# Softmax sums completed on VectorE, and output clearings tied to late pair loads, in a one-core attention and mixture-of-experts kernel

## The chip, the cores and the metric

The kernel runs on one core of one Trainium2 chip. The metric is the device time of one execution in microseconds (us), as the median of three runs. TensorE (PE) multiplies matrices, VectorE (DVE), ScalarE (ACT) and GpSimd (POOL) work element by element, and SyncE (SP) issues most of the memory transfers; GpSimd issues the indexed ones, which gather or scatter rows by a list of numbers. Each engine takes its instructions strictly in the order of its own queue, so an instruction that waits holds up everything behind it on that engine.

## The reference

Attention over eight batches of 576 positions with eight heads of 64, each position seeing itself and the 127 before it, and then a layer of eight experts of which every token takes the two best:

```python
scores = np.where(mask, scores + bias[None], -1000000000.0)
scores = scores - np.max(scores, axis=-1, keepdims=True)
attn = np.exp(scores)
attn = attn / (np.sum(attn, axis=-1, keepdims=True) + 1e-09)
...
noisy_logits = logits + noise_scale * noise
top2 = np.argpartition(-noisy_logits, 2, axis=1)[:, :2]
...
h = np.maximum(x[mask] @ w1[e], 0.0)
out[mask] += top2_w[mask, k, None] * (h @ w2[e])
```

## The kernel before, in words

The first part is attention. Its 32 pairs (a batch and two of its heads) are loaded one after the other (`qk`, line 452), each into one of four buffers. A pair is worked in three groups of query blocks: blocks 0 and 1, blocks 2 and 3, and the half block 4. A group passes through scores on PE (L498, or L491 for block 4), mask and maximum on DVE (L519, L524), the exponential on ACT, which leaves each row's sum in the tile `den` (L531), a transposition on PE (L538), its copy out of the bank by ACT or DVE (L266 or L270, tile `pT`), a split by two masks on GpSimd (L558, L559), and the product with the values on PE (L579).

When the four pairs of a batch have passed for one group, `rows` finishes it. The sums in `den` get 1e-9 added and are inverted. For block 4 the two heads of a pair lie on top of each other in the partitions, so that the sums of the lower half are first moved beside those of the upper half. Transposed rows (L681) are then multiplied by the inverted sums (L684) and stored as tokens in `xs`, and `gate` computes the experts' logits (L706, L717, L722, and the sum over heads on GpSimd, L731 and L732).

When a batch has all its logits, `route` picks two experts for every token, counts them (L782 to L787), makes lists (L822, L829) and adds them to the table `slots` in memory by an indexed transfer of GpSimd (`scatter`, L895 and L896). After the sixth batch (`CUT`) the first 768 tokens of expert 0 are gathered (L1157), made into two half-precision parts, turned by transposing transfers of SP (L1202) and fed to the first feed-forward blocks (L1210 up, L1254 down), which stand on PE between the last pieces of attention. The second part is feed-forward alone. Results are added to `out` by indexed transfers (L1343).

`out` and the spare rows of `xs` have to be cleared before that. `set_ups` does it with eleven transfers of 1 MB from a tile of zeros (L428), one after the other: one into `xs`, ten into `out`.

No queue's order is written by hand. A planner (`Order`) walks through all strands of work at build time with a cost for each piece and a rank that says which piece goes first; what it decides becomes the order of the queues. The ranks come from the numbers at the top (`LOAD` and `VALUES` for the loads of pairs and values, `GATE`, `ROUTE` and `SCATTER` for the end of a batch, `STAGE` for the steps of a group, `LATE` for choices between ACT and DVE).

Of the kernel before, what the change touches and what calls it, by code (L numbers as in the profile page):

```python
# [14 lines left out]
OP = mybir.AluOpType  # L15
# [3 lines left out]
B, H, S, D = 8, 8, 576, 64  # L19
# [17 lines left out]
NTR = 512  # L37
NPAD = N + NTR
BLOCKS = tuple(((FROWS, c - FROWS),) if z < NF else ((0, 512), (512, 384), (896, c - 896)) for z, c in enumerate(CAPS))
ZERO = 61.9  # L40
LOAD = -46.8
VALUES = 27.7
GATE = (-11.1, 102.8)
ROUTE = (6.1, 22.2)
SCATTER = (1.3, -1054.0, -21.3)
FFN0, FFN1 = 174.1, 232.3
WEIGHTS = (101.9, 86.4)
TOKENS = 85.5
STAGE = (-3.5, 6.3, 21.9, -7.2, 18.8, 32.3, 14.3, -20.1)
MIDDLE = 51.1  # L50
RESULT = -82.8
SIZES = (62.8, 73.0, 959.3)
SOON = 22.0
TIGHT = (1, 5, 7)
QUICK = (5, 7)
LATE = (-6.5, -40.7, 56.9, 77.5, 0.4, -92.0, 49.5, -132.3, 49.1, -25.4, 8.5, -39.8)
LAG = 0.2
TURN, MARGIN, LATE_BY = (1.4, 0.3), 1.0, 1.0
PACE, READ_BY, AHEAD = 4.0, 2.0, 16
HELD = 3  # L60
SWITCH, NEAR = 0.093, 6.2
TOP, SOFT, SPLIT = (1.27, 1.52, 0.46), (1.56, 1.56, 0.4), (0.85, 1.35, 0.6)
SP_COST = 0.45
DMA_RATE = 300e3
# [162 lines left out]
def attention_moe(ctx: ExitStack, tc: tile.TileContext, qk_, v, w_gate, w_noise, noise, w1, w2,  # L227
                  out, xs, slots, eye):
    nc = tc.nc
# [23 lines left out]
    def dve(us, rank, emit, join=True):  # L253
        return Op((("DVE", us, rank),), emit, join)

    def pool(us, rank, emit, join=True):
        return Op((("POOL", us, rank),), emit, join)
# [14 lines left out]
    def move(size, rank, emit):  # L272

        end = yield Op((("SP", SP_COST, rank),), emit)
        yield order.transfer(end, size)
# [12 lines left out]
    PAIRS = B * NP  # L288
# [84 lines left out]
    def set_ups():  # L373
        def small():
            nc.gpsimd.memset(base, 0)
            nc.gpsimd.memset(rest_of_line, 0)
            nc.gpsimd.memset(wgn, 0.0)
            for t in lgs:
                nc.gpsimd.memset(t, 0.0)
            nc.gpsimd.memset(caps, float(CAP))  # L380
            nc.gpsimd.memset(takes, 0.0)
            nc.gpsimd.iota(names, pattern=[[0, NQ], [1, E]], base=0, channel_multiplier=0,
                           allow_small_or_imprecise_dtypes=True)
            nc.gpsimd.memset(names[64:128, 4, :], 100.0)
            nc.gpsimd.iota(starts_, pattern=[[SPAN * LINE // 128, E]], base=0, channel_multiplier=0,
                           allow_small_or_imprecise_dtypes=True)
            nc.gpsimd.iota(iota8, pattern=[[1, E]], base=0, channel_multiplier=0,
                           allow_small_or_imprecise_dtypes=True)

        def counts_():  # L390
            for t, pattern, first_, step in ((steps_, [[1, E * SPAN]], 0, 0), (numbers, [[128, NQ]], 1, 1),
                                             (spare, [[128, 4]], N, 1), (mine, [[-SPAN, E]], 0, 1)):
                nc.gpsimd.iota(t, pattern=pattern, base=first_, channel_multiplier=step,
                               allow_small_or_imprecise_dtypes=True)
            nc.gpsimd.memset(numbers[64:128, 4:5], 0.0)
            nc.gpsimd.iota(first_line, pattern=[[0, 1]], base=0, channel_multiplier=1,
                           allow_small_or_imprecise_dtypes=True)

        def columns():
            reached = tmp[0:E * SPAN, 0]  # L400
            nc.vector.tensor_scalar(reached, mine, 0.0, None, op0=OP.is_ge)
            nc.vector.tensor_reduce(tmp[0:E * SPAN, 1, 0:1], reached[:, 1:E], axis=AX.X, op=OP.add)
            nc.vector.scalar_tensor_tensor(first_line, tmp[0:E * SPAN, 1, 0:1], float(LINES - SPAN), first_line,
                                           op0=OP.mult, op1=OP.add)
            nc.vector.scalar_tensor_tensor(mine, mine, float(SPAN), reached, op0=OP.is_lt, op1=OP.mult)
            nc.vector.tensor_copy(line_of[0], first_line)
            nc.vector.tensor_scalar(least[:, 0], iota8, float(NF), float(FROWS), op0=OP.is_lt, op1=OP.mult)

        yield pool(0.4, 2, small)
        yield pool(0.6, 4, counts_)  # L410
        yield pool(0.46, 5, lambda: nc.gpsimd.memset(zero, 0.0))
        for z, w in enumerate((w_gate, w_noise)):
            for h in range(2):
                yield from move(2e4, 6, lambda w=w, z=z, h=h: nc.sync.dma_start(
                    wgn[h * D:h * D + D, :, h * 16 + z * E:h * 16 + z * E + E],
                    dram(w, h * D * E, [[E, D], [128 * E, 4], [1, E]])))
        yield from move(2e5, 7, lambda: nc.sync.dma_start(noi, noise))
        yield dve(0.8, 7, columns)
        nt = E * EROWS // 128
        yield from move(2e5, 8, lambda: nc.sync.dma_start(dram(slots, 0, [[nt, 128], [1, nt]]), zero[:, 0:nt]))  # L420
        yield from move(1e4, 8, lambda: nc.sync.dma_start(eye, ident[0:E, 0:E]))
        mark(set_up)
        rest_ = NTR // 128 * XW - 4 * DM
        yield from move(2e4, 16, lambda: nc.sync.dma_start(
            dram(xs, N * XW + 4 * DM, [[4 * DM + rest_, 128], [1, rest_]]), zero[:, 0:rest_]))
        for z, (ap, r) in enumerate([(xs, N * XW)] + [(out, r * DM) for r in range(0, NPAD, 512)]):
            row_ = 4 * DM + (0 if z else rest_)
            yield from move(1e6, 16 + ZERO * z, lambda ap=ap, r=r, row_=row_: nc.sync.dma_start(  # L428
                dram(ap, r, [[row_, 128], [DM, 4], [1, DM]]), zero[:, None, :].to_broadcast([128, 4, DM])))
        put(xgr, zeros)  # L430
        mark(emptied)
# [5 lines left out]
    loaded = [Event() for _ in range(PAIRS)]  # L437
# [5 lines left out]
    def loads():  # L443

        for k in range(PAIRS):
            rank = 5 * k - LOAD
            t = qks[k] = yield (qkr, rank)
# [7 lines left out]
    def all_values():  # L455
        for y in range(2 * B):
            rank = 10 * y - VALUES
            if y == 0:
# [133 lines left out]
    def unit(u):  # L592
        k, gr = units[u]
        blocks = GROUPS[gr]
        t = k * NQ + blocks[0]
        r0, r1, r2, r3, r4, r5, r6, r7 = (t + z for z in STAGE)
        b, g, y = k // NP, k % NP, k // 2
# [40 lines left out]
        if g == NP - 1:  # L638
            spawn(rows(b, gr, t))
# [3 lines left out]
    def rows(b, gr, t):  # L643

        yield filled[b, gr]
        blocks, den = GROUPS[gr], dens[b, gr]
        nr, nz = 64 if blocks == (4,) else 128, len(blocks)
        rank = t - GATE[b + 1 == CUT]

        def sums():  # L650
            if nz == 1:
                nc.gpsimd.tensor_copy(den[0:64, 0, 1:H:2], den[64:128, 0, 0:H:2])
            nc.gpsimd.tensor_scalar(den[0:nr, 0:nz], den[0:nr, 0:nz], 1e-9, None, op0=OP.add)

        yield pool(0.4 if nz == 1 else 0.2, rank, sums)
        yield dve(0.2, rank, lambda: nc.vector.reciprocal(den[0:nr, 0:nz], den[0:nr, 0:nz]))
        done = Event(nz + 1)
        spawn(gate(b, blocks, xus[b, gr], den, t, done))
        for z, i in enumerate(blocks):
            spawn(row_major(b, i, xus[b, gr][:, :, z * 128:z * 128 + nr], den[0:nr, z], t + z, done))  # L660
        yield done
        put(xur[nz == 1], xus[b, gr])
        put(denr, den)
# [8 lines left out]
    def row_major(b, i, xu, den, t, done):  # L672

        rank = t - GATE[b + 1 == CUT]
        rows = 64 if i == 4 else 128
# [19 lines left out]
    def gate(b, blocks, xu, den, t, done):  # L695


        rank = t - GATE[b + 1 == CUT]
        nz, i = len(blocks), blocks[0]
# [51 lines left out]
    def route(b):  # L751
# [146 lines left out]

        rank = 20 * b + SCATTER[2 if b == B - 1 else b + 1 == CUT]
        yield pool(1.08, rank, scatter)  # L900
# [151 lines left out]
    def say(e):  # L1052
# [6 lines left out]
        yield begun[e - 1]  # L1059
        yield Op((("SP", 1.5, SIZES[2] + step_of(e) - 1),), load)  # L1060
        mark(known[e])
# [9 lines left out]
    def early_sizes():  # L1071

        yield biased[NP - 1]
        for e in range(EARLY):
            done = Event(16)
            for f in range(8):
                for z, (rg, src) in enumerate(((raw1, w1), (raw2, w2))):
                    t = yield (rg, SIZES[e])
                    v = t.rearrange("p a b -> p (a b)") if z == 0 else t
                    spawn(largest(rg, t, v, (0.6, 0.7)[z], SIZES[e], wam[:, e % 2, z, f:f + 1],  # L1080
                                  dram(src, e * DM * F + f * 65536, [[512, 128], [1, 512]]), done, z))
            yield done
            yield from powers_of_weights(e, SIZES[e])

# [149 lines left out]
    def middle(blk, f, t, rank, end):  # L1234
        c = blk.n
        yield end
        if f == 7:
# [4 lines left out]
        blk.h[f][1].extend((hh, hl))  # L1242
        yield either(0.052 + c * 0.000833, 0.067 + c * 0.00104, rank - MIDDLE, LATE[8], lambda e: relu(
            e, hh[:, 0:c], t[:, 0:c]))
        yield dve(0.07 + c * 0.00104, rank - MIDDLE, lambda: nc.vector.scalar_tensor_tensor(  # L1245
            hl[:, 0:c], t[:, 0:c], 0.0, hh[:, 0:c], op0=OP.max, op1=OP.subtract))
# [114 lines left out]
    def first_tokens():  # L1361
        for z, blk in enumerate(first):
            yield from tokens(blk, ranks1[8 * z] - TOKENS)

# [257 lines left out]
```

## Time and profile before

| | |
|---|---|
| Median of three runs | 1075.29 us (1074.47 to 1076.39) |
| Profiled execution, its own time | 1074.38 us |
| Span of its profile, first to last instruction | 1072.6 us |
| Busy: PE, DVE | 1025.2 us (96%), 681.9 us (64%) |
| Busy: ACT, GpSimd | 444.4 us (41%), 391.1 us (36%) |
| Mean granted PE clock | 0.982 of 2.4 GHz |

The time is 1.8 us longer than the span. The shares are averages over two parts with different habits: in the first 275 us all four compute engines work on attention, afterwards PE is almost never idle. The granted clock is the share of 2.4 GHz that PE was given; 0.50 stands for 1.2 GHz.

### The profile page before, as it was taken

The page shows a single profiled execution, that of the slowest core. Times are in us where ns is not written, and L with a number is a line of the kernel's source. Part 1 is how long each engine was busy: PE and PEld are TensorE (multiplying, and loading weights), DVE is VectorE, ACT ScalarE, POOL GpSimd, SP SyncE. Part 2 cuts the span into 40 slices and gives each one's busy share as a digit, 9 for nine tenths or more (in the row PEclk, how much of TensorE's full clock was granted, in tenths as well). Part 3 has the DMA queues.
Part 4 walks back from the last instruction along what each step waited for, and adds up shares of the span by engine and source line. Part 5 has one row for each costly group of instructions (what it writes and reads, how often), then busy time and mean ns, then how long its engine had stood idle before and what let it go on. Part 6 is the DMA issues. An engine that isn't in the chain of part 4 may idle for free. (4 is left out here: it accounts for less than half of the span.)

```text
span 1072.6 us, 20479 instructions
## 1 busy us (share of the span) xinstructions
PE 1025.2 (96%) x6880; PEld 604.6 (56%) x6880; DVE 681.9 (64%) x2402; ACT 444.4 (41%) x1265; POOL 391.1 (36%) x660
## 2 busy tenths in 40 slices
PE   8997997888998999999999999999999999999996
PEld 5765665555554554564457456645744574574454
DVE  8987996678747765665666676546755664673311
ACT  8986785556223342333333234314423331442211
POOL 4466775676442130332213142205222330431112
PEclk9999998899999999999999999999999999999998
DMA  8889785525368994979479868948894797787113
GB/s 304 303 293 315 224 304 186 157 71 145 91 169 185 181 193 132 192 126 219 101 151 213 187 79 188 190 132 170 141 241 63 180 187 184 139 132 90 23 35 48
DMA packets 193307, 178.62 MB, mean 167 GB/s; under 512 B 104048, under 2 KB 147344, under 8 KB 193200
## 3 DMA queue, kind: packets, MB, share of 16 engines
q1 hardware_dynamic: 175856, 138.34, 48.0%
q0 software_dynamic: 17344, 38.94, 22.7%
q8 instruction: 55, 0.90, 0.4%
q14 instruction: 52, 0.43, 0.1%
HBM read 117.29 MB, written 40.71 MB: 147 GB/s over the span
## 5 line engine op out<-in xcount | busy, mean ns | idle before, releaser
L1343 POOL DMA_INDIRECT out_dram<-yo,ix x71 | 114.9, 1618 | 504.3 <-ACT yo L266 491.9
L1230 ACT ACTIVATE hh<-bank 128x384 f16<-128x384 f32 (+9 forms) x177 | 87.6, 495 | 435.3 <-PE bank L1210 415.5
L1245 DVE SCALAR_TENSOR_TENSOR hl<-bank,hh 128x384 f16<-128x384 f32 (+9 forms) x192 | 107.8, 561 | 233.3 <-ACT hh L1230 225.6
L1254 PEld LDWEIGHTS <-hh 128*128 128x128 f16 x912 | 89.2, 98 | 96.2
L1210 PE MATMUL bank<-xh,w1hb 128*128 128x512 f16 (+8 forms) x384 | 126.5, 329 | 0.0
L1210 PE MATMUL bank<-xl,w1hb 128*128 128x512 f16 (+8 forms) x384 | 126.5, 329 | 0.0
L1210 PE MATMUL bank<-xh,w1lb 128*128 128x512 f16 (+8 forms) x384 | 126.4, 329 | 0.0
L531 ACT ACTIVATE p<-p,nm 128x128 f32<-128x128 f32 x288 | 111.7, 394 | 14.9 <-DVE nm L524 14.8
L1210 PE MATMUL bank<-xl,w1ha 128*128 128x384 f16 (+8 forms) x320 | 105.6, 330 | 0.0
L1210 PE MATMUL bank<-xh,w1la 128*128 128x384 f16 (+8 forms) x320 | 105.6, 330 | 0.0
L1210 PE MATMUL bank<-xh,w1ha 128*128 128x384 f16 (+8 forms) x320 | 105.6, 330 | 0.0
L1210 PEld LDWEIGHTS <-w1hb 128*128 128x128 f16 x768 | 74.8, 98 | 53.7
L1210 PEld LDWEIGHTS <-w1ha 128*128 128x128 f16 x768 | 74.6, 98 | 53.6 <-issue 0.3
L1157 POOL DMA_INDIRECT xg<-xs_dram,ix x71 | 79.7, 1123 | 40.7 <-issue 13.9
L1254 PE MATMUL bank<-w2ha,hl 128*128 128x512 f16 x228 | 86.6, 380 | 3.3 <-DVE hl L1245 1.8
L1254 PE MATMUL bank<-w2hb,hl 128*128 128x512 f16 x228 | 86.5, 380 | 0.2 <-DVE hl L1245 0.2
L1254 PE MATMUL bank<-w2hb,hh 128*128 128x512 f16 x228 | 86.5, 380 | 0.0
L1254 PE MATMUL bank<-w2ha,hh 128*128 128x512 f16 x228 | 86.5, 380 | 0.0
L1254 PE MATMUL bank<-w2lb,hh 128*128 128x512 f16 x228 | 86.5, 379 | 0.0
L1254 PE MATMUL bank<-w2la,hh 128*128 128x512 f16 x228 | 86.5, 379 | 0.0
L579 PE MATMUL bank<-pT,vraw 128*64 128x128 f32 (+2 forms) x896 | 76.1, 308 | 10.5 <-POOL pT L559 7.7
L1115 DVE TENSOR_REDUCE wam<-mraw 128x1 f32<-128x1024 f32 x56 | 66.9, 1210 | 21.0 <-DMA mraw<-in_w_dram 21.0
(242 smaller groups left out, 2029.7 us busy)
## 6 DMA issues: line engine op xcount, KB each, us to landing
raw<-in_w_dram SPq DMA_DIRECT2D x144, 256.0 KB
mraw<-in_w_dram SPq DMA_DIRECT2D x56, 512.0 KB
qk<-in_qk_dram SPq DMA_DIRECT2D x32, 608.0 KB
vraw<-in_v_dram SPq DMA_DIRECT2D x16, 640.0 KB
out_dram<-xg SPq DMA_DIRECT2D x10, 1024.0 KB
xs_dram<-x SPq DMA_DIRECT2D x32, 256.0 KB
xg<-xs_dram,ix POOLq DMA_INDIRECT x71
xh<-th SPq DMA_TRANSPOSE x71
```

The costliest lines, as they stand in the source:

```text
L531: nc.scalar.activation(pv, pv, AF.Exp, bias=nm[:, z, h:h + 1], scale=-1.0, accum_out=den[:, z, 2 * g + h:2 * g + h + 1])
L579: nc.tensor.matmul(o[half, o0:o0 + c], t[:, kb, hh:hh + D], w, start=m == 0, stop=m == len(lst) - 1)
L1115: yield dve(us, rank, lambda: nc.vector.tensor_reduce(o, v, axis=AX.X, op=OP.max, apply_absolute_value=True))
L1157: yield pool(1.04, rank, lambda: nc.gpsimd.indirect_dma_start(out=xg[0:r], out_offset=None, in_=xs[0:blk.rows], in_offset=bass.IndirectOff ...
L1210: nc.tensor.matmul(t[:, 0:blk.n], wp[:, c], x[:, c, 0:blk.n], start=c == 0 and z == 0, stop=c == 3 and z == 2)
L1230: nc.scalar.activation(o, i, AF.Relu)
L1245: yield dve(0.07 + c * 0.00104, rank - MIDDLE, lambda: nc.vector.scalar_tensor_tensor(hl[:, 0:c], t[:, 0:c], 0.0, hh[:, 0:c], op0=OP.max, ...
L1254: nc.tensor.matmul(blk.y[j][0:r], h[:, cs], wp, start=f == 0 and m == 0, stop=f == 7 and m == 2)
L1343: ins = nc.gpsimd.indirect_dma_start(out=out, out_offset=bass.IndirectOffsetOnAxis(ap=blk.ix[0:r, j:j + 1], axis=0), in_=t[0:r], in_offset ...
```

## The change

The sums' arithmetic moves from GpSimd to DVE and is written as one piece with the inversion. For groups of two blocks it is one addition of 1e-9 and one reciprocal. For block 4 the move of the lower half and its addition are one instruction (L653 of the changed file), the upper half's addition another (L654), and the reciprocal follows. Each of the eleven clearings gets a wait: number z (from 0) may be planned only once pair 18 + z (from 0) has been loaded (`PAIRS + EMPTY + z`). A dozen of the planner's numbers change as well (`LOAD`, `VALUES`, `GATE`, `SCATTER`, `FFN0`, `FFN1`, `TOKENS`, `STAGE`, `MIDDLE`, `SIZES`, `LATE`, `NEAR`).

```diff
-ZERO = 61.9
-LOAD = -46.8
-VALUES = 27.7
-GATE = (-11.1, 102.8)
+ZERO, EMPTY = 61.9, -14
+LOAD = -36.5
+VALUES = 43.7
+GATE = (-11.1, 96.6)
...
-SCATTER = (1.3, -1054.0, -21.3)
-FFN0, FFN1 = 174.1, 232.3
+SCATTER = (55.8, -1054.0, -31.5)
+FFN0, FFN1 = 184.2, 258.7
...
+            yield loaded[PAIRS + EMPTY + z]
             yield from move(1e6, 16 + ZERO * z, lambda ap=ap, r=r, row_=row_: nc.sync.dma_start(
...
             if nz == 1:
-                nc.gpsimd.tensor_copy(den[0:64, 0, 1:H:2], den[64:128, 0, 0:H:2])
-            nc.gpsimd.tensor_scalar(den[0:nr, 0:nz], den[0:nr, 0:nz], 1e-9, None, op0=OP.add)
-
-        yield pool(0.4 if nz == 1 else 0.2, rank, sums)
-        yield dve(0.2, rank, lambda: nc.vector.reciprocal(den[0:nr, 0:nz], den[0:nr, 0:nz]))
+                nc.vector.tensor_scalar(den[0:64, 0, 1:H:2], den[64:128, 0, 0:H:2], 1e-9, None, op0=OP.add)
+                nc.vector.tensor_scalar(den[0:64, 0, 0:H:2], den[0:64, 0, 0:H:2], 1e-9, None, op0=OP.add)
+            else:
+                nc.vector.tensor_scalar(den, den, 1e-9, None, op0=OP.add)
+            nc.vector.reciprocal(den[0:nr, 0:nz], den[0:nr, 0:nz])
+
+        yield dve(0.55 if nz == 1 else 0.35, rank, sums)
```

In the rows of the built programs below, the words in brackets are the semaphores an instruction waits on: DMASW is a transfer that GpSimd issued, DMAHW one that SP issued, the others are engines.

GpSimd's queue before, at the first batch's scatter into `slots` and the block-4 sums of the second batch:

```order
L896 DMA slots_dram<-listed_182,line_of_153 704x64 [waits DMAHW4_49,DVE_49]
L731 TENSOR_TENSOR lt_117<-lt_117 64x64 [waits DVE_49]
L731 TENSOR_TENSOR lt_117<-lt_117 64x32 [waits Pool_49]
L732 TENSOR_TENSOR lg_166<-lt_117 64x16 [waits Pool_49]
L652 COPY den_106<-den_106 64x4 [waits DMASW0_49]
L653 TENSOR_SCALAR den_106<-den_106 64x8 [waits Pool_49]
L558 AFFINE_SELECT pT_96<-pT_96 128x2x128 [waits Activation_49]
L559 AFFINE_SELECT pT_96<-pT_96 128x2x128 [waits PE_49,Pool_49]
```

The same place of GpSimd's queue after the change:

```order
L559 AFFINE_SELECT pT_98<-pT_98 128x128 [waits Activation_49]
L560 AFFINE_SELECT pT_98<-pT_98 128x128 [waits Pool_49]
L898 MEMSET pad 1x1
L899 DMA slots_dram<-listed_182,line_of_153 704x64 [waits DMAHW1_49,DVE_49]
L559 AFFINE_SELECT pT_95<-pT_95 128x2x128 [waits DVE_49]
L560 AFFINE_SELECT pT_95<-pT_95 128x2x128 [waits PE_49,Pool_49]
L769 TENSOR_SCALAR u_186<-y_185 128x40 [waits Activation_49]
```

Before, the copy of `den` waits on DMASW0, and the splits of `pT` stand behind it. After, no `den` instruction is left on GpSimd, and the splits follow the scatter directly. The waits on earlier scatters that the copies carried are now on the scatters of later batches, as DMASW0 on the second batch's.

DVE's queue before, at the same block-4 sums, and then after:

```order
L524 ISA p_85,nm_89<-bank_69,bias 128x128 [waits PE_49]
L524 ISA nm_89 128x1
L656 RECIPROCAL den_106<-den_106 64x8 [waits Pool_49]
L1146 SCALAR_TENSOR_TENSOR w2la_217<-raw_124,wsc,w2ha_216 128x512 [waits DMAHW6_49]
L519 COPY_PREDICATED bank_66<-own_key,bank_66 128x2x128 [waits PE_49]
```

```order
L725 TENSOR_TENSOR lt_116<-bank_73,den_111 128x256 [waits PE_49]
L653 TENSOR_SCALAR den_106<-den_106 64x4
L654 TENSOR_SCALAR den_106<-den_106 64x4
L657 RECIPROCAL den_106<-den_106 64x8 [waits DVE_49]
L520 COPY_PREDICATED bank_66<-own_key,bank_66 128x128
```

The reciprocal waited for GpSimd; now two additions stand ahead of it on its own engine, without a wait.

SP's queue before, at the third clearing of `out`, and then after, at the first two clearings:

```order
L689 DMA xs_dram<-x_112 128x512
L944 DMA xs_dram<-gd_181 128x4x8
L428 DMA out_dram<-xg_129 512x1x512
L689 DMA xs_dram<-x_113 64x512
L452 DMA qk_79<-in_qk_dram 128x1216
```

```order
L947 DMA xs_dram<-gd_199 128x4x8
L429 DMA xs_dram<-xg_129 128x4x512
L463 DMA vraw_82<-in_v_dram 128x5x256
L453 DMA qk_81<-in_qk_dram 128x1216
...
L692 DMA xs_dram<-x_114 64x512
L429 DMA out_dram<-xg_129 512x1x512
L453 DMA qk_79<-in_qk_dram 128x1216
```

The third clearing of `out` stood ahead of the 18th pair's load. Now the clearing of `xs` comes after the 19th, and the ten of `out` follow one by one between the later loads, the last of them behind the 32nd.

## Rows read from the trace of the kernel before

**Rows 1.** Windows by stage: length, busy time by engine, granted clock, DMA share, GB/s.

```profile
0.00:107.30 107.30, 95.04 (x896) 66.58 (x897) 88.22 (x472) 89.00 (x377) 57.83 (x157) 0.98 0.89 304
107.30:214.50 107.20, 97.07 (x966) 65.80 (x968) 85.75 (x460) 71.58 (x305) 69.84 (x168) 0.92 0.66 218
...
345.50:1062.50 717.00, 715.98 (x4110) 402.37 (x4108) 412.58 (x1061) 229.77 (x404) 193.41 (x209) 1.00 0.73 146
```

**Rows 2.** Waits from 5 to 275 us: who waited for whom, total, times, longest.

```profile
DVE den L656 <- POOL den L653: 16.9, 7, 5.5
...
POOL den L652 <- DMA slots_dram<-listed,line_of: 12.6, 4, 4.3
...
PE bank L498 <- DMA qk<-in_qk_dram: 4.9, 1, 4.9
```

**Rows 3.** Timeline at 93 to 103 us: start, duration, engine, line, idle before and releaser.

```profile
93.11 2.98 POOL L896 DMA_INDIRECT slots_dram<-listed,line_of  x1 [0.98 <-DVE lt L722]
...
101.34 0.18 POOL L652 COPY den<-den 64x4 f32<-64x4 f32 x1 [4.28 <-DMA slots_dram<-listed,line_of]
...
101.89 0.20 DVE L656 RECIPROCAL den<-den 64x8 f32<-64x8 f32 x1 [5.50 <-POOL den L653]
...
103.20 1.12 PE L579 MATMUL bank<-pT,vraw 128*64 128x256 f32 x4 [5.00 <-POOL pT L559]
```

**Rows 4.** Timeline at 169 to 172 us.

```profile
169.46 0.18 POOL L652 COPY den<-den 64x4 f32<-64x4 f32 x1 [3.69 <-DMA slots_dram<-listed,line_of]
...
170.02 0.19 DVE L656 RECIPROCAL den<-den 64x8 f32<-64x8 f32 x1 [5.11 <-POOL den L653]
...
171.00 0.69 DVE L270 COPY pT<-bank 128x512 f32<-128x512 f32 x1
...
171.74 1.12 PE L681 MATMUL bank<-ident,xu 128*128 128x128 f32 x4 [5.20 <-DVE pT L270]
```

**Rows 5.** Timeline at 201 to 204 us.

```profile
201.38 0.18 POOL L652 COPY den<-den 64x4 f32<-64x4 f32 x1 [3.97 <-DMA slots_dram<-listed,line_of]
...
201.92 0.20 DVE L656 RECIPROCAL den<-den 64x8 f32<-64x8 f32 x1 [2.50 <-POOL den L653]
...
203.60 0.36 ACT L266 ACTIVATE gt<-bank 128x256 f32<-128x256 f32 x1
...
204.01 1.11 PE L681 MATMUL bank<-ident,xu 128*128 128x128 f32 x4 [3.65 <-ACT gt L266]
```

**Rows 6.** Windows just behind those three places, columns as in rows 1.

```profile
103.20:108.20 5.00, 5.00 (x34) 3.48 (x36) 3.43 (x17) 2.42 (x11) 4.39 (x14) 0.71 0.84 312
...
171.70:176.90 5.20, 5.16 (x32) 3.64 (x32) 5.20 (x33) 1.74 (x9) 3.12 (x7) 0.50 0.14 52
...
204.00:209.00 5.00, 4.71 (x25) 3.15 (x27) 3.92 (x25) 1.35 (x4) 4.13 (x14) 0.50 0.28 105
209.00:214.00 5.00, 5.00 (x50) 3.51 (x52) 3.61 (x22) 3.12 (x18) 2.53 (x8) 0.71 0.12 22
```

**Rows 7.** DVE groups by form, 60 to 275 us: count, busy us, mean ns, idle before.

```profile
L794 DVE TENSOR_SCALAR line<-base 128x8 int32<-128x8 int32 x6 | 1.0, 165 | 0.0
...
L766 DVE TENSOR_SCALAR u<-y 128x40 f32<-128x40 f32 x1 | 0.3, 309 | 0.0
```

**Rows 8.** A window of attention without such a place, columns as in rows 1.

```profile
110.00:165.00 55.00, 54.43 (x577) 37.40 (x574) 51.27 (x268) 47.06 (x201) 40.49 (x93) 1.00 0.81 264
```

**Rows 9.** GpSimd's additions by source line: shortest, median, longest in ns.

```profile
L653 POOL TENSOR_SCALAR den<-den x24: 229/266/700, 32.8 to 270.5; 128x16 f32<-128x16 f32 x16, 64x8 f32<-64x8 f32 x8
```

**Rows 10.** Loads of pairs issued by 83 us: count, shortest, median, longest, first and last start.

```profile
L452 SPq DMA_DIRECT2D qk<-in_qk_dram x17: 327/339/573, 0.8 to 82.4; - x17
```

**Rows 11.** Score matmuls that began by 114.7 us (sixteen records a pair).

```profile
L498 PE MATMUL bank<-qk x256: 271/376/632, 4.9 to 110.0; 64*128 64x256 f32 x94, 64*128 64x128 f32 x34
```

**Rows 12.** Window of the last 49 us of attention, columns as in rows 1.

```profile
226.00:275.00 49.00, 38.18 (x348) 25.19 (x347) 38.74 (x178) 28.12 (x112) 34.86 (x68) 0.90 0.43 107
```

**Rows 13.** Timeline: the first feed-forward matmul.

```profile
275.07 0.33 PE L1210 MATMUL bank<-xhe,w1ha 128*128 128x384 f16 x1
```

More of the change, by code (lines that the diff above doesn't have):

```diff
@@ L39 @@
 BLOCKS = tuple(((FROWS, c - FROWS),) if z < NF else ((0, 512), (512, 384), (896, c - 896)) for z, c in enumerate(CAPS))
-ZERO = 61.9
-LOAD = -46.8
-VALUES = 27.7
-GATE = (-11.1, 102.8)
+ZERO, EMPTY = 61.9, -14
+LOAD = -36.5
+VALUES = 43.7
+GATE = (-11.1, 96.6)
 ROUTE = (6.1, 22.2)
-SCATTER = (1.3, -1054.0, -21.3)
-FFN0, FFN1 = 174.1, 232.3
+SCATTER = (55.8, -1054.0, -31.5)
+FFN0, FFN1 = 184.2, 258.7
 WEIGHTS = (101.9, 86.4)
-TOKENS = 85.5
-STAGE = (-3.5, 6.3, 21.9, -7.2, 18.8, 32.3, 14.3, -20.1)
-MIDDLE = 51.1
+TOKENS = 98.7
+STAGE = (-3.5, 5.1, 17.1, -7.2, 18.8, 32.3, 14.3, -20.1)
+MIDDLE = 74.9
 RESULT = -82.8
-SIZES = (62.8, 73.0, 959.3)
+SIZES = (67.4, 72.1, 971.4)
 SOON = 22.0
@@ L55 @@
 QUICK = (5, 7)
-LATE = (-6.5, -40.7, 56.9, 77.5, 0.4, -92.0, 49.5, -132.3, 49.1, -25.4, 8.5, -39.8)
+LATE = (-6.5, -40.7, 56.9, 103.9, -16.3, -92.0, 32.0, -132.3, 99.3, -25.4, 51.6, -39.8)
 LAG = 0.2
@@ L60 @@
 HELD = 3
-SWITCH, NEAR = 0.093, 6.2
+SWITCH, NEAR = 0.093, 7.0
 TOP, SOFT, SPLIT = (1.27, 1.52, 0.46), (1.56, 1.56, 0.4), (0.85, 1.35, 0.6)
```

## The prediction

> **What bounds the kernel now.** I read the windows by stage first, to see where PE could gain anything [rows 1]. From 345.5 to 1062.5 us PE is busy 715.98 of 717.00 us at full clock: the feed-forward part has no slack to give, and whatever comes earlier in front of it moves its end by the same amount. In the first 107.3 us PE is idle 12.3 us, in the next 107.2 us 10.1 us, and there its granted clock is 0.98 and 0.92. No other engine is full either: DVE is at 82% and 80%. So attention is limited by waits between queues.
>
> The list of waits names them [rows 2]. GpSimd sat 12.6 us in front of the copy of `den` (L652), four times, until the transfer that adds lists to `slots` had landed. DVE sat 16.9 us in front of the reciprocal (L656), for GpSimd's addition. The copy reads nothing of that transfer; the built program has a wait on it all the same, as GpSimd's queue before the change shows. Why it is put there, no trace tells, but its price can be followed in the timelines. At 93.11 us the scatter is issued; the copy stands still for 4.28 us until 101.34; the splits of `pT` are queued behind it, and PE, which needs a split, is idle for 5.00 us until 103.20. DVE waits 5.50 us in front of its reciprocal [rows 3]. The second time DVE waits 5.11 us; the copy of `pT` behind the reciprocal is late, and PE is idle 5.20 us [rows 4]. The third time GpSimd waits 3.97 us, the chain goes on through gate tiles, and PE is idle 3.65 us [rows 5]. The fourth of the four waits is what remains, 12.6 - 4.3 - 3.7 - 4.0 = 0.6 us, too little to follow.
>
> Behind each of these pauses PE works at a lower granted clock [rows 6]: 0.71 for 5 us after the first, 0.50 (that is the 1.2 GHz level) for 5.2 us after the second, 0.50 and then 0.71 after the third.
>
> **The change part by part.** *The stall goes.* In the changed program GpSimd has no `den` instruction, and DVE's three carry no wait on a transfer. The waits on a scatter now sit on the next batch's scatter, a batch later. So three idle spells of PE go: 5.00 + 5.20 + 3.65 = 13.85 us [rows 3 to 5]. What is late next in those places? At the first, DVE itself was busy only until it met the reciprocal; everything waited on the one copy. I therefore take the whole idle time.
>
> *The clock behind them.* Work done at a granted clock c would take c times as long at full clock, so what it costs is busy time by (1 - c): 5.00 x 0.29 + 5.16 x 0.50 + 4.71 x 0.50 + 5.00 x 0.29 = 1.45 + 2.58 + 2.36 + 1.45 = 7.84 us [rows 6]. It presumes that PE sets the pace there; the bound below is nothing, if ACT or DVE set it.
>
> *Additions on DVE.* 16 groups of two blocks get one addition, 8 half blocks two: 32 instructions. The trace has no DVE addition of this shape. The nearest rows are an operation on 8 elements a partition, 165 ns, and one on 40 elements, 309 ns [rows 7]; the added ones have 16 or 4. So 32 x 0.165 = 5.3 us to 32 x 0.309 = 9.9 us, and I take 5.3, since the sizes lie by the shorter row. Where attention runs undisturbed PE is busy 99% and DVE 93% [rows 8]; DVE is close to being the pace, not at it. I put half on the path, 2.6 us; the bounds are 0 and 9.9.
>
> *DVE no longer waits for GpSimd's addition.* Of 16.9 us in seven waits, 5.50 + 5.11 + 2.50 = 13.11 lie in the three places above. The other four waits, 3.8 us, were also in DVE's queue; again half, 1.9 us, with bounds 0 and 3.8. On GpSimd 24 additions of 0.266 us go [rows 9], 6.4 us of an engine that is busy 40.49 of 55 us [rows 8]; their worth is the splits' coming earlier, which is counted with the stall already, so nothing more.
>
> *Clearings.* Eleven transfers of 1 MB keep their number and size and come later, between the loads of pairs 19 to 32. In the first 107.3 us the transfers moved 304 GB/s, in the next 107.2 us 218 [rows 1]; one clearing takes about 1.0/304 = 3.4 us of that. PE's only wait for a pair is the one of 4.9 us before its first scores [rows 2], so moving them out of the early, crowded stretch brings nothing I can price, and moving them into the later one costs nothing as long as pairs are loaded well ahead. They are: the 17th load is issued at 82.4 us [rows 10], and by 114.7 us PE has begun the scores of only sixteen pairs [rows 11], so a pair waits about 30 us in its buffer or on the way. That lead is the cover; a lost cover is a rival below.
>
> *The planner's numbers.* In the orders, PE's work keeps its sequence nearly everywhere; the first feed-forward matmul and the second part stand where they stood, give or take a few pieces. The last 49 us of attention lose 49.0 - 38.2 = 10.8 us of PE to idle time and 38.18 x 0.10 = 3.8 us to the clock [rows 12], spread over small waits. Some may go as GpSimd loses work, others may come; I count zero, with bounds of +14.6 and the same again in loss.
>
> *Sum.* 13.85 + 7.84 - 2.6 + 1.9 = 21.0 us. It comes off the profiled execution, 1074.4 us (span 1072.6, with 1.8 around it, which the tail keeps); that execution is 0.9 us under the median of the three. That gives **1053.4 us**, which I round to 1053. The saving has to survive until the feed-forward part begins. The first of its matmuls ran at 275.07 us [rows 13] right behind attention's own work, so it was not waiting for its tokens; moved forward as a whole, with routing and gathering moved too, it keeps that.
>
> **The rivals.** *Ports.* DVE and GpSimd now meet more often on small tiles, and either can make the other wait. GpSimd's additions lasted 229 to 700 ns for the same work [rows 9], so something already stretches them. If each of the 32 additions costs its upper price on the path, 9.9 us, and the clock behind the old stalls gives only half, 3.9 us, the time is 1074.4 - 13.85 - 3.9 + 9.9 = 1066.5. For it: DVE's 93%. Against: the additions are short, and the path's other engine, PE, is as full. Chance 0.17. The Trainium skill, "SBUF — State Buffer", section "Who interferes with whom", speaks against this change: a tensor-scalar instruction on VectorE whose data lie in SBUF can take the port pair that it shares with GpSimd, and then blocks GpSimd for its whole length. By that rule the blocked time on GpSimd would be the additions' own 5 to 10 us, spread over 24 places; no row here shows an addition of `den` on VectorE, and a spread of 229 to 700 ns is what the rule would make, without proving it.
>
> *More than the stalls goes.* If half of what the last 49 us lose, 7.3 us, vanishes too, and all 3.8 us of DVE's waits and none of the additions count, the time is 1074.4 - 13.85 - 7.84 - 3.8 - 7.3 = 1041.6. For it: GpSimd is freed and its scatter no longer carries splits behind a copy. Against: in the last stretch routing is a long chain of its own, which ends in the gathered tokens and cannot shrink by taking additions away. Chance 0.13.
>
> *It does not do what it says.* The wait on the scatter reappears with the same length elsewhere on GpSimd, for instance on the scatter after it. Then 1074. Against: scatters are 30 us apart, their landing took at most 101.34 - 93.11 = 8.2 us [rows 3]. Chance 0.03.
>
> *Slower: loads behind clearings.* If the later pairs' loads come just in time, every clearing queued ahead of one delays PE by 3.4 us; for all eleven that is 37 us, and the time 1053.4 + 37 = 1090. It outweighs the gain from the seventh clearing on (7 x 3.4 = 24 us). For it: the planner now puts them between just those loads, and compressed attention needs them sooner. Against: the lead of about 30 us. Chance 0.07, in which I include a time over 1077.
>
> **How the numbers follow.** The forecast, 1045 to 1061, has 0.60. Leaving out the far part of each rival, the range that should hold 8 in 10 goes from 1040 (the second rival with its bound) to 1067 (the first). A measurement of this kernel tells about 0.2% from no change, some 2 us. Faster comes from the forecast and the first two rivals, 0.90, less 0.01 for their far ends: 0.89. Same: 0.03, and slower: 0.08.
>
> **What would show it.** Right: no L652 and no wait of GpSimd for the `slots` transfer in front of anything but a scatter; no idle spell of PE over 3 us between 90 and 210 us; granted clock above 0.97 in the second stage; the first feed-forward matmul at about 254 us; after it the same spacing as before. The additions show as L653, L654 and L656 on DVE with 0.15 to 0.3 us each. Wrong: an idle PE in front of scores with a load as releaser (clearings); splits stretched over their present length while DVE adds (ports); the first feed-forward matmul idle for its tokens, which would mean that the saving was given back there.

## The result and the profile after

The changed kernel takes 1057.07 us, the median of four runs (1054.98 to 1057.37), against 1075.84 us for the kernel before in the same comparison (1074.47 to 1077.24). The ratio is 0.9821 with a 95% interval of 0.9803 to 0.984, so it is faster by 18.8 us. The forecast was 1053 us with a range of 1040 to 1067. The profiled execution took 1054.98 us with a span of 1053.2 us, 19.4 us less than that of before.

Windows by stage of the kernel after, in the columns of [rows 1]; the stages end at its own first feed-forward matmul (251.65 us), at the start of the second part (324.1) and at the last matmul, and the last row is a stretch at a low clock:

```profile
0.00:251.60 251.60, 232.38 (x2348) 160.81 (x2349) 230.55 (x1218) 199.50 (x831) 161.50 (x381) 0.99 0.76 249
0.00:107.30 107.30, 101.16 (x999) 71.27 (x1001) 95.54 (x523) 93.25 (x388) 60.10 (x162) 1.00 0.76 258
107.30:214.50 107.20, 100.31 (x1054) 68.89 (x1054) 100.98 (x534) 83.05 (x356) 75.01 (x168) 1.00 0.83 281
214.50:251.60 37.10, 30.91 (x299) 20.65 (x298) 34.02 (x165) 23.21 (x89) 26.39 (x53) 0.95 0.55 131
251.60:324.10 72.50, 68.12 (x426) 36.15 (x424) 45.80 (x157) 15.19 (x31) 24.21 (x38) 0.98 0.60 149
324.10:1043.30 719.20, 716.45 (x4110) 402.95 (x4108) 411.81 (x1058) 230.10 (x407) 194.21 (x209) 1.00 0.71 146
...
248.20:255.00 6.80, 5.70 (x49) 3.76 (x50) 6.45 (x31) 1.02 (x3) 4.57 (x11) 0.50 0.68 99
```

Three windows of the kernel before that end, or begin, at the same places of the work: its first feed-forward matmul [rows 13] and the start of its second part:

```profile
0.00:275.10 275.10, 241.89 (x2341) 165.69 (x2342) 223.52 (x1176) 198.28 (x829) 169.99 (x406) 0.94 0.70 227
214.50:275.10 60.60, 49.78 (x484) 33.30 (x481) 49.55 (x246) 37.69 (x149) 42.32 (x83) 0.92 0.41 107
275.10:345.50 70.40, 67.13 (x433) 36.52 (x431) 45.84 (x166) 15.63 (x33) 25.42 (x44) 1.00 0.62 157
```

This is the balance. Up to the first feed-forward matmul the changed kernel is 23.5 us shorter. Of that, 33.2 - 19.2 = 14.0 us is idle time of PE and 241.9 - 232.4 = 9.5 us is PE being busy for less time, at a granted clock of 0.99 instead of 0.94. The first part of feed-forward then takes 72.50 us instead of 70.40, and the second 719.20 instead of 717.00 [rows 1]. So 4.3 us of the gain are given back behind attention.

Waits of the kernel after from 5 to 275 us, in the columns of [rows 2]:

```profile
POOL lt L734 <- DVE lt L725: 11.6, 9, 3.3
...
PE bank L499 <- DMA qk<-in_qk_dram: 4.8, 1, 4.8
...
POOL slots_dram L899 <- DVE listed L833: 2.4, 1, 2.4
```

No instruction on `den` waits in the list any more, no compute instruction waits for the transfer into `slots`, and PE waits for a pair's load once, at the start, as it did before.

Its timeline at the scatter, at the first feed-forward matmul and at the two longest pauses of the first feed-forward part, in the columns of [rows 3]:

```profile
90.04 1.68 POOL L899 DMA_INDIRECT slots_dram<-listed,line_of  x1 [0.57 <-PE bank L539]
...
91.21 0.94 POOL L559 TENSOR_SCALAR_AFFINE_SELECT pT<-pT 128x256 f32<-128x256 f32 x1
...
251.65 0.53 PE L1213 MATMUL bank<-xhe,w1ha 128*128 128x384 f16 x1
...
302.34 0.39 PE L1257 MATMUL bank<-w2ha,hh 128*128 128x512 f16 x1 [1.80 <-DVE fit L484]
...
320.30 0.39 PE L1257 MATMUL bank<-w2ha,hl 128*128 128x512 f16 x1 [1.41 <-DVE hl L1248]
```

A split follows the scatter without a pause, where 4.28 us lay before [rows 3]. Between 90 and 210 us no idle spell of PE is longer than 0.74 us.

DVE groups by form of the kernel after, over the whole run, in the columns of [rows 7]:

```profile
L656 DVE TENSOR_SCALAR den<-den 128x16 f32<-128x16 f32 x16 | 3.7, 231 | 0.0
L654 DVE TENSOR_SCALAR den<-den 64x4 f32<-64x4 f32 x8 | 1.6, 202 | 0.1
...
L653 DVE TENSOR_SCALAR den<-den 64x4 f32<-64x4 f32 x8 | 1.5, 186 | 0.2
```

The 32 additions last 6.8 us together.

### The profile page after: what moved, and what is told of

Read it like the earlier page. It is cut to its first block, busy times and chain, and to the rows that moved or that the text cites. A ratio compares the mean times of both kernels' runs of the same rounds, so it can differ in the third digit from the quotient of the medians.

```text
span 1053.2 us, 20482 instructions
## 1 busy us (share of the span) xinstructions
PE 1017.3 (97%) x6880; PEld 599.9 (57%) x6880; DVE 688.2 (65%) x2430; ACT 445.5 (42%) x1269; POOL 382.4 (36%) x628
## 5 line engine op out<-in xcount | busy, mean ns | idle before, releaser
L1257 PEld LDWEIGHTS <-hl 128*128 128x128 f16 x456 | 44.8, 98 | 60.8 <-DVE hl L1248 8.5
L580 PE MATMUL bank<-pT,vraw 128*64 128x128 f32 (+2 forms) x896 | 72.3, 297 | 4.9 <-POOL pT L560 4.6
```

Source lines behind the costliest of these rows:

```text
L580: nc.tensor.matmul(o[half, o0:o0 + c], t[:, kb, hh:hh + D], w, start=m == 0, stop=m == len(lst) - 1)
L1257: nc.tensor.matmul(blk.y[j][0:r], h[:, cs], wp, start=f == 0 and m == 0, stop=f == 7 and m == 2)
```

## The experiments

The theory: the one copy of `den` behind the scatter is the whole gain; the clearings and the planner's numbers bring nothing; the additions cost about half their length. The rivals: the clearings or the new order of the work carry the gain, or the additions on DVE cost much more. Each kernel was timed beside the kernel before on the same chip (medians of 1077.43, 1075.35 and 1075.22 us in the three groups), so that the ratios are what to compare.

**The sums alone, and everything but the sums.** `sums_only` is the kernel before with the new sums, under the old numbers and with the early clearings:

```diff
-        yield pool(0.4 if nz == 1 else 0.2, rank, sums)
-        yield dve(0.2, rank, lambda: nc.vector.reciprocal(den[0:nr, 0:nz], den[0:nr, 0:nz]))
+        yield dve(0.55 if nz == 1 else 0.35, rank, sums)
```

> The kernel before with the sums' arithmetic on VectorE and nothing else: old numbers of the planner, clearings early. Theory (the removed wait of GpSimd on the scatter is the whole gain): 1054 to 1061 us, about 16 to 21 us under before, and no idle spell of PE over 3 us between 90 and 210 us. Rival (the later clearings or the planner's new numbers hold a good part of it): 1065 us or more.

`all_but_sums` is the kernel after with that edit turned round.

> The changed kernel with the sums' arithmetic back on GpSimd: new numbers and late clearings stay. Theory (the removed wait is the whole gain): 1070 to 1080 us, with idle spells of PE of 3 to 6 us behind the copy of den. Rival (clearings and numbers): 1057 to 1066 us.

Without the sums nothing is left of the gain: 1077.39 us, ratio 1.001 (0.9991 to 1.0028). Its timeline shows the old chain at its old place, and its windows up to the first feed-forward matmul and from there to the last one:

```profile
98.09 0.18 POOL L653 COPY den<-den 64x4 f32<-64x4 f32 x1 [4.32 <-DMA slots_dram<-listed,line_of]
...
99.94 1.12 PE L580 MATMUL bank<-pT,vraw 128*64 128x256 f32 x4 [4.86 <-POOL pT L560]
```

```profile
0.00:269.10 269.10, 239.01 (x2335) 166.10 (x2336) 230.41 (x1195) 196.00 (x824) 168.26 (x410) 0.94 0.73 233
269.10:1064.70 795.60, 785.37 (x4547) 440.36 (x4546) 455.74 (x1205) 248.94 (x443) 218.64 (x248) 1.00 0.71 145
```

Here the copies wait for a scatter in only two places, 8.7 us in all. The first feed-forward matmul comes at 269.1 us, 6.0 us earlier than before, but the rest takes some 8 us longer (795.6 us against 787.2, from the first feed-forward matmul to the last). So without the moved sums the new order shortens attention a little and lengthens what follows by as much.

With the sums alone the time is 1067.69 us (eight executions from 1060.99 to 1071.98), ratio 0.9912 (0.988 to 0.9944). That is half of the gain, outside the 1054 to 1061 us of the theory and inside the rival's 1065 us or more: with all the sums moved, the old numbers hold half of the gain back. The timeline of `sums_only` and its windows show where:

```profile
242.38 0.68 DVE L1180 TENSOR_REDUCE fit<-xg 128x1 f32<-128x512 f32 x1
...
244.46 0.42 DVE L724 TENSOR_TENSOR lt<-bank,den 128x256 f32<-128x256 f32 x1
...
244.93 1.29 PE L538 MATMUL bank<-ident,p 128*128 128x128 f32 x3 [6.10 <-DVE lt L724]
```

```profile
0.00:254.90 254.90, 232.97 (x2297) 162.00 (x2298) 229.53 (x1201) 194.71 (x818) 156.63 (x368) 0.96 0.76 245
254.90:1055.40 800.50, 789.74 (x4584) 442.82 (x4583) 461.70 (x1236) 249.00 (x444) 221.66 (x259) 1.00 0.70 145
```

The three old spells are gone here too. But the planner, with another cost for the sums, put work on the gathered tokens (among it their maxima, `fit`, L1180) ahead of an operation of the gate for which PE then stood 6.10 us. The first feed-forward matmul comes at 254.9 us, 20.2 us earlier than before, though some of that is work put off: 2297 matmuls stand ahead of it instead of 2341. From there to the last matmul it takes 13.3 us longer than before. Half of that is idle time, 10.8 us instead of 4.3, with two pauses behind DVE of 3.85 and 3.32 us at 306 and 349 us; the other half is busy time, for some 40 matmuls more. So 6.9 us of the 20.2 are there at the last matmul. The loss comes with the order, not with the additions' length: `no_late_clear`, next, has the same additions and clearings under the new numbers and is 11 us faster.

**The clearings.** `no_late_clear` is the kernel after without the clearings' wait:

```diff
-            yield loaded[PAIRS + EMPTY + z]
```

> The changed kernel without the wait of the clearings, so that they go early again as before; sums on VectorE and the new numbers stay. Theory (the wait of GpSimd is the whole gain): 1054 to 1060 us, as the changed kernel within 3 us. Rival (the early clearings crowd the loads, and moving them brings part of the gain): 1062 us or more. Rival on the other side (late clearings get in the way of the last loads): 1051 us or less.

It took 1056.28 us, ratio 0.981 (0.9783 to 0.9836): no difference from the kernel after that its interval would show. Its ten clearings of `out` are issued from 59.4 to 161.8 us, those of the kernel after from 117.9 to 205.6, in either case with one wait of PE for a load, of 4.8 us at the start. The place of the clearings is worth nothing that can be told from noise, some 3 us.

**The copy alone.** `shift_on_dve` is the kernel before with only the eight copies moved; the 24 additions stay on GpSimd, with the old numbers:

```diff
-            if nz == 1:
-                nc.gpsimd.tensor_copy(den[0:64, 0, 1:H:2], den[64:128, 0, 0:H:2])
...
+        if nz == 1:
+            yield dve(0.2, rank, lambda: nc.vector.tensor_copy(den[0:64, 0, 1:H:2], den[64:128, 0, 0:H:2]))
+        yield pool(0.2, rank, sums)
```

> The kernel before with only the eight copies that move the lower half's sums taken from GpSimd to VectorE; all 24 additions stay on GpSimd, the reciprocal still waits for them, numbers and clearings as before. Theory (the wait that sat on the copy is the whole gain): 1054 to 1062 us. Rival (taking the additions off GpSimd and out of VectorE's wait is a good part): 1066 us or more.

It took 1058.12 us, ratio 0.9822 (0.9802 to 0.9842): the whole gain with 8 of the 32 instructions. DVE still waits for GpSimd's additions, 1.8 us in three times instead of 16.9 in seven [rows 2]. So the additions as such never held DVE up for long; what they stood behind did.

**The copy put back.** `copy_back` is the kernel after with a copy of the same shape on GpSimd between two halves of a tile that nobody reads, at each finish of block 4:

```diff
+        if nz == 1:
+            yield pool(0.2, rank, lambda: nc.gpsimd.tensor_copy(idle_[0:64], idle_[64:128]))
```

> The changed kernel with eight copies of a 64x4 tile that nothing uses, from the upper to the lower half of the partitions, put on GpSimd where block 4 of a batch is finished; in the built program they wait on the scatter as the copies of den did. Theory (that wait alone makes the difference): GpSimd again idle some 12 us in front of them, PE idle 10 to 15 us in front of matmuls behind the splits, 1068 to 1080 us, most of the change undone although the sums stay on VectorE and do not need these copies. Rival (the sums' path through GpSimd and back was the cost, not the wait): 1055 to 1061 us.

It took 1060.7 us, ratio 0.9851 (0.9825 to 0.9876), and the 1068 to 1080 us of the theory were missed. GpSimd's groups by form say why:

```profile
L661 POOL COPY idle<-idle 64x4 f32<-64x4 f32 x8 | 1.9, 243 | 1.0 <-DMA slots_dram<-listed,line_of 0.6
```

The copies that follow a scatter came to stand 6.6 to 11 us behind its start, and the transfer had nearly landed by then: 0.6 us of waiting in all eight. (The other 3 us over the kernel after come with a new order of the work, below.) So the dose had to be set by hand. `copy_close` puts a copy directly behind three of the scatters, and every queue keeps the order of the kernel after:

```diff
+            if b in (0, 2, 3):
+                nc.gpsimd.tensor_copy(idle_[0:64], idle_[64:128])
```

> The changed kernel, every queue's order the same, with three copies of an unused 64x4 tile between the partitions' halves on GpSimd directly behind the scatters of the first, third and fourth batch; in the built program each waits on its scatter. Theory (such a wait, close behind the scatter, is what the kernel before lost its time to): GpSimd idle 4 to 6 us in front of each, PE idle 3 to 5 us behind each, lower clock behind that, 1072 to 1082 us. Rival (splits and PE catch up, the wait alone costs little): 1057 to 1064 us.

It took 1074.49 us (1067.79 to 1076.38), ratio 0.9977 (0.9954 to 0.9999) to the kernel before: three copies of 0.18 us undo nearly all of the gain. The timeline of `copy_close`:

```profile
90.13 1.68 POOL L900 DMA_INDIRECT slots_dram<-listed,line_of  x1 [0.57 <-DVE pT L270]
96.39 0.18 POOL L903 COPY idle<-idle 64x4 f32<-64x4 f32 x1 [4.58 <-DMA slots_dram<-listed,line_of]
96.65 0.41 POOL L560 TENSOR_SCALAR_AFFINE_SELECT pT<-pT 128x256 f32<-128x256 f32 x1
...
101.14 0.69 PE L721 MATMUL bank<-ident,gt 128*128 128x128 f32 x2 [5.26 <-DVE x L688]
```

Its list of waits, and its window up to the first feed-forward matmul at 267.7 us:

```profile
POOL idle L903 <- DMA slots_dram<-listed,line_of: 13.7, 3, 5.4
```

```profile
0.00:267.70 267.70, 240.18 (x2348) 165.32 (x2349) 229.64 (x1219) 199.46 (x831) 161.31 (x385) 0.95 0.73 234
```

The copy reads a tile that only one fill at the start has written, and it stands still until the scatter has landed, 13.7 us in three times. Against the kernel after PE is idle 8.3 us longer and busy 7.8 us longer at a clock of 0.95: the two halves of the gain, brought back by the copy alone. Its idle spells of PE are 5.26, 3.87 and 3.77 us, where [rows 3 to 5] have 5.00, 5.20 and 3.65.

**The additions.** `adds_more` is the kernel after with 48 more additions, of zero, in front of the reciprocals; the other instructions keep their order in every queue:

```diff
+            for _ in range(2):
+                nc.vector.tensor_scalar(den[0:nr, 0:nz], den[0:nr, 0:nz], 0.0, None, op0=OP.add)
             nc.vector.reciprocal(den[0:nr, 0:nz], den[0:nr, 0:nz])
```

> The changed kernel with two more passes over the sums in each of the 24 places, adding zero: 48 more additions on VectorE, the planner's costs and so the order unchanged. Prediction's price (half of the additions' own 0.24 us on the path): 48 x 0.24 x 0.5 = 6 us, 1061 to 1065 us. Hidden: 1056 to 1059. All on the path: 1067 to 1070. By the rule of the Trainium skill on the shared port pair, GpSimd's splits would last longer beside them.

DVE groups by form of `adds_more`:

```profile
L658 DVE TENSOR_SCALAR den<-den 128x16 f32<-128x16 f32 x32 | 7.3, 227 | 1.1
...
L658 DVE TENSOR_SCALAR den<-den 64x8 f32<-64x8 f32 x16 | 3.1, 194 | 0.5
```

It took 1065.54 us, ratio 0.9903 (0.9877 to 0.9929): 8.5 us more than the kernel after for 10.4 us of additions, 0.18 us each or some 80% of their length, where I had put half. By the intervals of the two ratios it can be 0.11 to 0.25 us each, so half is at the edge of what the runs allow. The first feed-forward matmul comes 8.6 us later, so the cost arises in attention.

**The planner's numbers.** Four kernels ask whether the numbers do anything of their own. `sums_cheap` is `sums_only` with the old cost of 0.2 for the piece; `old_middle` is the kernel after with three old numbers that bear on the feed-forward part (`MIDDLE`, and 49.5 and 49.1 in two places of `LATE`); `shift_new_numbers` is the kernel after with the sums of `shift_on_dve`; `near_old` is the kernel after with one old number (`NEAR`).

```diff
-        yield dve(0.55 if nz == 1 else 0.35, rank, sums)
+        yield dve(0.2, rank, sums)
...
-MIDDLE = 74.9
+MIDDLE = 51.1
...
-SWITCH, NEAR = 0.093, 7.0
+SWITCH, NEAR = 0.093, 6.2
```

> The run with only the sums moved, but the planner told 0.2 us for the piece on VectorE instead of 0.35 or 0.55: the same instructions with old numbers in another order. Theory (the 10 us that the run with only the sums lacked come from a bad arrangement behind attention, not from the additions): the time moves by several us, to between 1055 and 1063, and the idle spell of 6 us in front of a transposition at 239 us is gone or elsewhere. Rival (the additions on VectorE cost them): 1066 to 1070 us.

> The changed kernel with the three numbers that rank the work between the two feed-forward matrices set back (MIDDLE 51.1, LATE[6] 49.5, LATE[8] 49.1). Theory (they are why the feed-forward part lasts 4 us longer than before): 1051 to 1054 us, with the stretch from the first feed-forward matmul to the last back at 787 us. Rival (the 4 us are an accident of order that any number moves): 1056 to 1062 us.

> The changed kernel with its new numbers and late clearings, but only the copy of the lower half's sums on VectorE; the 24 additions stay on GpSimd. By the price of an addition on VectorE (0.18 us each from the run with 48 more): 24 fewer of them give 4 us, 1051 to 1055 us. Rival (the arrangement decides a few us either way): 1056 to 1066 us.

> The changed kernel with one of the planner's small numbers set back (NEAR 6.2 for 7.0), which alters the order of some thousands of rows but no work. If the arrangement alone moves the time by several us: anywhere from 1052 to 1067, off 1057 by 3 us or more. If not: within 2 us of 1057.

`sums_cheap` took 1065.12 us (ratio 0.9898, 0.9872 to 0.9923), between what the theory and the rival said. The spell of 6.10 us is gone, and one of 4.48 us stands at 240.8 us instead; this tells nothing certain of the cost. `old_middle` took 1059.5 us (0.9831, 0.98 to 0.9862) and gains back nothing in the feed-forward part, so those three numbers are not what gives the 4.3 us back. `shift_new_numbers` took 1063.06 us (0.9881, 0.9859 to 0.9903), slower than the same edit under the old numbers; I had expected the fewer additions on DVE to show as 1051 to 1055. `near_old` took 1060.52 us (0.9856, 0.9833 to 0.9879), 3.5 us more than the kernel after for the same work in another order. So these kernels, which differ from the kernel after in order above all, lie 1 to 8 us over it by their ratios, with no direction that the numbers explain. What the new numbers are worth depends on the edit they go with: nothing without the moved sums (`all_but_sums`), 11 us with all the sums moved (from `sums_only` to `no_late_clear`, 0.9912 to 0.981), and a loss of some 6 us with the copy alone (from `shift_on_dve` to `shift_new_numbers`, 0.9822 to 0.9881). Differences of that size between re-planned kernels are read as order; only `copy_close` and `adds_more`, whose queues stand as in the kernel after, give a price.

## Why the prediction was right, and where it was off

*The stall goes: right.* The three spells were priced at 13.85 us and the clock behind them at 7.84. With the two smaller terms that made 13.15 us of idle time and 7.84 of clock. Measured up to the first feed-forward matmul: 14.0 us of idle time and 9.5 us of PE's busy time; how much of that lies where the sum looked is worked out below. `shift_on_dve` and `copy_close` tie it to one instruction, from both sides: 17.4 us more when a copy is put behind three of the scatters, about 19 us less when the copies are taken away. Why the program has the wait on the copy stays open. In the built programs GpSimd's copies from one half of the partitions to the other carry it, also between tiles that the transfer does not touch, as `copy_close` shows, while the additions in place do not; no run here tells what the rule is.

*A wait's price depends on its distance.* The prediction took four waits in front of L652 for three stalls, and `copy_back` shows that this was no chance: eight copies of the same shape, a few microseconds further behind the scatters, wait 0.6 us.

*The additions: mis-sized.* The term was "I put half on the path, 2.6 us". The additions last 6.8 us instead of 5.3. A nearer row than the two of [rows 7] was there, the reciprocal on the same tile, in DVE's groups by form of the kernel before:

```profile
L656 DVE RECIPROCAL den<-den 128x16 f32<-128x16 f32 x16 | 3.9, 244 | 3.4 <-POOL den L653 3.4
L656 DVE RECIPROCAL den<-den 64x8 f32<-64x8 f32 x8 | 1.5, 184 | 13.6 <-POOL den L653 13.5
```

It gives 16 x 0.244 + 16 x 0.184 = 6.8 us. What part lies on the path is less sure. At the price of `adds_more` 32 additions would cost 32 x 0.18 = 5.7 us, an estimate: that price was measured for additions on top of these, and no run takes these away and leaves the order. DVE was "close to being the pace, not at it" at 93% in the window without stalls that the prediction read [rows 8]; with the stalls gone the whole second stage is like that window, 101.0 of 107.2 us or 94%, against 80% before [rows 1].

*The last stretch of attention: put at nothing, 2.4 us.* From 214.5 us to the first feed-forward matmul PE is idle 6.2 us, in the kernel before from the same time on 10.8 us, but the first stretch holds 299 matmuls and the second 484. Counted back over the same number of matmuls, the kernel after begins at 193.4 us:

```profile
193.40:251.60 58.20, 48.98 (x483) 33.16 (x484) 53.86 (x270) 38.47 (x155) 42.27 (x85) 0.97 0.57 156
```

It needs 58.2 us with 9.2 us of idle time, where the kernel before needed 60.6 with 10.8. So 2.4 us were gained there, and the second rival ("half of what the last 49 us lose", 7.3 us) hardly happened. The other 21.1 of the 23.5 us came earlier, where the sum had 21.0: 12.4 us of idle time for its 13.15, and 8.7 us of busy time for its 7.84. This balance leaves no room for additions at 5.7 us instead of 2.6, unless another 3 us were gained that no run shows.

*The saving carries through: the step that failed.* The text said that it "has to survive until the feed-forward part begins" and then keeps, with "the same spacing as before" after it. Of 23.4 us only 19.0 reach the last matmul (1062.3 to 1043.3 us). In the first feed-forward part 1.1 us are more idle time (4.4 against 3.3): the 1.80 and 1.41 us behind DVE shown above were there before too, with 1.50 and 1.39 us, so most of it is smaller pauses, of 0.55 and 0.48 us and less. And 1.0 us is more busy time at a clock of 0.98: the granted clock is 0.50 from 248.2 to 255.0 us, from the third of three idle spells of PE (1.62, 1.26 and 1.75 us) on, and so reaches over the start of feed-forward. In the second part idle time grows from 1.02 to 2.75 us, in spells of at most 0.69 us, most of them before matmuls that read `hl`, which DVE writes; another 0.5 us is busy time. Where it goes is measured; why DVE is later for `hl` is not settled. `old_middle` rules out three of the numbers as its reason. In none of the twelve changed kernels is the way from the first feed-forward matmul to the last as short as before (787.2 us); they need 789.6 (`shift_on_dve`) to 800.6 us (`sums_only`), so how much is lost goes with the order. That the forecast lies within 2 us of the profiled execution (1053.4 and 1054.98 us) is therefore partly luck: the 2.4 us left out in front of feed-forward and the 4.3 us lost behind it go against each other.

*Clearings at nothing: right*, by `no_late_clear`. The lead was there: 17 loads are issued by 82.8 us, as before [rows 10], and no load but the first ends a wait of PE in attention.

*The rivals.* The slower one (loads behind clearings) did not happen. Nor did the wait reappear elsewhere: GpSimd waits for that transfer in front of no compute instruction. *Ports:* the spread that the prediction read, 229 to 700 ns, mixes two shapes: 229 to 246 ns for 64x8, and 252 to 700 for 128x16. In the kernel after the first splits of a pair became longer. GpSimd's groups by form of the kernel before, then after, then of `adds_more`, then of `sums_only`:

```profile
L558 POOL TENSOR_SCALAR_AFFINE_SELECT pT<-pT 128x512 f32<-128x512 f32 x32 | 20.5, 641 | 16.9 <-ACT pT L266 11.6 <-DVE pT L270 4.3 <-PE bank L538 0.8
```

```profile
L559 POOL TENSOR_SCALAR_AFFINE_SELECT pT<-pT 128x512 f32<-128x512 f32 x32 | 23.7, 740 | 17.6 <-ACT pT L266 13.8 <-DVE pT L270 2.3 <-PE bank L580 1.4
```

```profile
L559 POOL TENSOR_SCALAR_AFFINE_SELECT pT<-pT 128x512 f32<-128x512 f32 x32 | 23.2, 724 | 18.5 <-ACT pT L266 12.8 <-PE bank L580 3.3 <-DVE pT L270 2.3
```

```profile
L558 POOL TENSOR_SCALAR_AFFINE_SELECT pT<-pT 128x512 f32<-128x512 f32 x32 | 21.4, 670 | 17.8 <-ACT pT L266 14.1 <-PE bank L538 1.9 <-DVE pT L270 1.4
```

They go from 641 to 740 ns, but 48 more additions on DVE leave them at 724, and `sums_only`, with the same 32 additions in another order, has 670. A price that grows with the additions is not there; the long splits go with the order of the kernel after, and what in it stretches them is not settled. The Trainium skill, "SBUF — State Buffer", section "Who interferes with whom", would have a split blocked for as long as an addition on DVE that took the shared ports first runs. A longer split in the kernel after agrees with that, the splits in `adds_more` and `sums_only` do not, so the runs leave the rule unproven for instructions this short.

## What to carry to other kernels

Look in the list of waits for a compute instruction that waits for a transfer it has nothing to do with: on an engine that works in order, copies of 0.18 us each, close behind three or four indexed transfers, cost 17 to 19 us here, somewhat more than half in idle time and the rest in the clock after it, and they cost next to nothing where they came 6.6 us or more after the transfer's start. To price such a wait, put a useless copy of the instruction at the suspected place and leave all else in order; re-planned kernels differ by several microseconds for their order alone. A saving in an early part is not safe in a later one that has no slack of its own: read the time at which the later part starts and the time at which it ends apart.

## What was not expected of the hardware

A GpSimd copy of 64 x 4 numbers between two halves of a tile that no transfer touches stood still for 5.4 us at the longest, until an indexed transfer issued just ahead of it had landed. Short additions on DVE spread widely for the same shape: L653 lasts 164 to 309 ns, and L656 154 to 606 ns with a median of 172, though their mean of 231 ns is what the queue pays. And pauses of PE of only 1.3 to 1.8 us, three of them, went with 6.8 us at a granted clock of 0.50, where the single pause of 5.20 us was followed by 5.2 us or more at that clock [rows 4, 6].
